# Attention and gated FFN on one core: one group's input sums in five parts, another first bank for the one-unit group, one state copy on VectorE

## The chip, the core and the metric

The kernel runs on one core of one Trainium2 chip. The metric is device time in microseconds (us) of one execution. Five engines work side by side, each in the order of its own instruction list: TensorE (PE in the profile, its weight loads PEld), VectorE (DVE), ScalarE (ACT), GpSimd (POOL) and SyncE (SP), which here only issues DMAs. They wait for each other through semaphores. An engine that waits holds up everything behind it in its list.

## The reference

A causal linear attention with decay, in blocks of 64 positions, for 4 batches, 8 heads, 768 positions and a head size of 64:

```python
for b in range(nb):
    intra = einsum(qb, kb) * Dmask[None]            # scores inside the block, decayed and masked
    intra = einsum(intra, vb)
    inter = einsum(qb * lam_pow[None], kv_state)    # all earlier blocks, through a 64 x 64 state
    out[:, :, sl] = intra + inter
    kv_state = lam_block * kv_state + einsum(kb * rev_pow, vb)
```

Its output, as a matrix x of 3072 tokens by 512, goes through a gated layer with 1536 hidden columns:

```python
a = x @ w_a
b = x @ w_b
return (a * b @ w_out)
```

All inputs are drawn at random in float32, and the output is float32.

## The kernel before

**Units and groups.** A unit is 128 tokens of one batch with all heads; there are 24, six to a batch. They are taken in eight groups of 4, 1, 2, 4, 4, 4, 4 and 1 units (`GROUPS`). The attention of a unit writes its result, transposed and in bf16, into a tile `xT` of its group; the gated layer of a group reads that tile. While the layer of group g runs, the attention of later units is slipped in between its matmuls: after each step the layer calls `hook(slot)`, and the table `PLAN[g]`, written by hand, says which pieces are emitted at which slot. There is no other scheduler: each engine works in the order in which the code emits.

**Pieces.** `P` prepares a unit (scaling of q and k on POOL, the transposing DMA, v to bf16), `S` its scores and masks, `V` updates the running state, `O2` makes the outputs of two units and copies them to `xT` in two halves on ScalarE (`evac_o`, L520: the first copy writes two of the four blocks of 128 rows, the second the others). For later pairs `O2` also updates the state beside it (`kv_beside`, L549) and copies it for the next unit (`kv_copy`): on VectorE as one multiply with a block mask (L560), or on ScalarE as two copies (L558); the table `KV_ENG` says which. `X` makes the sums of a group's x (`x_sums`, L701).

**The layer of groups 3 to 6.** It uses a Strassen-like scheme with seven products of half size in place of eight (`ffn_z`). They need sums of quarters of x: `z_sub` (1024 columns per partition), `z_add` (1024) and `z_mix` (512), made once per group, and sums of the weights. For each of six steps n, products are accumulated in PSUM banks named U (bank 0 or 1 in turn), V and W; ScalarE copies two or three partial results out (`snap`, L812), VectorE subtracts them from later ones (L760 to L777), a last product into U follows in the next step, ScalarE copies it (L737) and VectorE multiplies the two factors (L739, tile `ab`). In group 3 a step begins: U from `xT`, V from the first half of `z_sub`, W from the first half of `z_add`, then U from `z_mix` (which must wait until the first U has been copied), then V from the other half of `z_add`. In groups 5 and 6 the output products of the group before are slipped in too (`H`, L853; their input sums are `SM`, L826 to L832), and V and W share a bank. The sums of group 6 (`X`, 6) are made by POOL.

**The output of group 3** is plain (`out_plain`, L793): four tiles, each copied by ScalarE into one of the three buffers of `o_pool` (L638) and stored by a DMA that SyncE issues (L639).

**SyncE's list** holds in emission order the loads of q, k and v (L187), the transposing DMAs (L429) and the stores.

**Banks.** PSUM has eight banks; one holds the state. `ps_bank` hands out the others in rotation from a counter `bank["next"]`, leaving out those in `bank["held"]`. While groups 3 to 6 run, banks 0 to 4 are held, and 5 and 6 serve the attention. The last group, one unit, uses the ordinary layer `ffn` (`a_part` and `b_part`: tiles a_ps and b_ps, L596) in rotation over banks 0, 1, 2, 5 and 6, while 3 and 4 take the output products of group 6. Just before it the pending last product of group 6 is emitted:

```python
            bank["held"] = {3, 4} if fin else set()
            if fin:
                fin.pop()()
            ffn(g_u0[g], n, gx.pop(g), hook, g == 0, g + 1 == len(GROUPS))
```

Of the kernel before, what the change touches and what calls it, by code (L numbers as in the profile page):

```python
# [17 lines left out]
BF16 = mybir.dt.bfloat16  # L18
# [4 lines left out]
def _bc(ap, dims):  # L23
# [58 lines left out]
Z_GROUPS = (3, 4, 5, 6)  # L82
# [10 lines left out]
                        [0] +  # L93
                        [1] +
                        [0] * 2))
KV_ENG = dict(enumerate(["dve"] * 10 + ["act"] * 2 + ["dve"] + ["act"] * 11))
VB_ENG = dict(enumerate(["pool"] * 7 +
                        ["dve"] * 3 +
                        ["pool"] * 5 +
# [14 lines left out]
def kernel(  # L114
# [11 lines left out]
    nc = tc.nc  # L126
# [20 lines left out]
    xz_pool = ctx.enter_context(tc.tile_pool(name="xz", bufs=4))  # L147
# [11 lines left out]
    bank = {"next": 0, "held": set(), "ffn": None}  # L159
# [12 lines left out]
    def z_bank(name, i):  # L172
        return ps_pool.tile([128, 2, 256], F32, name=name, tag=f"ps{i}")
# [57 lines left out]
    def cast_w(kind, c, eng):  # L231
        t, slot = staged.pop((kind, c))
        if slot is not once:
            slots.append(slot)
        if kind == "o":
            dst = wo_sb[:, 2 * c:2 * c + 2, :]
        else:
            dst = w_part(wa_sb if kind == "a" else wb_sb, c)
        if eng == "act":
            nc.scalar.copy(dst, t)  # L240
        elif eng == "pool":
            nc.gpsimd.tensor_copy(dst, t)
        elif eng == "first":
            nc.vector.tensor_copy(dst[:, :3, :128], t[:, :3, :128])  # L244
            nc.gpsimd.tensor_copy(dst[:, 3:, :128], t[:, 3:, :128])
            nc.gpsimd.tensor_copy(dst[:, :, 128:], t[:, :, 128:])
        elif eng == "both":
            nc.vector.tensor_copy(dst[:, :, :128], t[:, :, :128])
            nc.scalar.copy(dst[:, :, 128:], t[:, :, 128:])
        elif eng == "cols":  # L250
            nc.vector.tensor_copy(dst[:, :, :128], t[:, :, :128])
            nc.vector.tensor_copy(dst[:, :, 128:], t[:, :, 128:])
        else:
            nc.vector.tensor_copy(dst, t)
        pump()
# [73 lines left out]
    gx, xTs = {}, {}  # L329
    g_u0 = [sum(GROUPS[:i]) for i in range(len(GROUPS))]  # L330

    def new_xT(g):
        gx[g] = xT_pool.tile([128, KS, 512], BF16, name="xT", tag="xT")
        for i in range(GROUPS[g]):
            xTs[g_u0[g] + i] = (gx[g], i * BLK)
# [61 lines left out]
    def eng_of(name):  # L397
        return nc.gpsimd if name == "pool" else nc.vector
# [35 lines left out]
    def prep_v(u):  # L434
        make_vb(u, VB_ENG[u])
        pump()
# [116 lines left out]
    def kv_copy(u, ps, eng="dve"):  # L553
        st = st_bufs[u % 4]
        if eng == "act":
            for b in range(2):
                p = slice(64 * b, 64 * b + 64)
                nc.scalar.copy(st[p, :, b, :], ps[p, :, b, :])  # L558
        else:
            nc.vector.tensor_mul(st[:].rearrange("p c b d -> p c (b d)"),  # L560
                                 ps[:].rearrange("p c b d -> p c (b d)"), bdiag_bc)

    def piece_S(u):
        masks(u, scores(u))

    def piece_V(u):
        kv_update(u)
        if u % NB < NB - 1:
            kv_copy(u, kv["ps"], KV_ENG[u])

    def pieces_O(us, nxt=()):
# [15 lines left out]
        if beside and us[1] % NB < NB - 1:  # L587
            kv_copy(us[1], kv["ps"], KV_ENG[us[1]])

# [37 lines left out]
    def store_kept():  # L627
        row, o_sb = kept.pop(0)
        nc.sync.dma_start(out=out_r[row], in_=o_sb)
# [68 lines left out]

    xz = {}

    def x_sums(g):  # L701
        xT = gx[g]
        z_add = xz_pool.tile([128, 2, 512], BF16, name="z_add", tag="xz")
        z_sub = xz_pool.tile([128, KS, 256], BF16, name="z_sub", tag="xz")
        z_mix = mix_pool.tile([128, 2, 256], BF16, name="z_mix", tag="z_mix")
        eng_of(XS_ENG[g, 0]).tensor_sub(z_sub, xT[:, :, 0:256], xT[:, :, 256:512])
        eng_of(XS_ENG[g, 1]).tensor_add(z_add, xT[:, 0:2, :], xT[:, 2:4, :])
        eng_of(XS_ENG[g, 2]).tensor_add(z_mix, xT[:, 0:2, 0:256], xT[:, 2:4, 256:512])
        xz[g] = (z_add, z_sub, z_mix)

    fin = []
    pairs = [0]
# [97 lines left out]
    def snap(ps):  # L810
        t = snap_pool.tile([128, 2, 256], F32, name="u", tag="snap")
        nc.scalar.copy(t, ps)  # L812
        return t
# [22 lines left out]
    def out_half(g, i):  # L836
        d = outs[g]
        p, h = O_ORDER[i // 2], i % 2
        ab = d["ab"]
        lhs = {0: ab[:, NP:, 256:], 1: ab[:, :NP, 256:], 2: ab[:, NP:, :256], 4: ab[:, :NP, :256]}  # L840
        if p in (3, 5, 6):
            lhs[p] = d["z"][:, 1 if p == 6 else 0]
        rhs = wo_sums.get(p)
        if rhs is None:
            rhs = wo_sb[:, :NP, :HN] if p == 1 else wo_sb[:, NP:, HN:]
        c = "U" if p in (1, 5, 3, 2) else "V"
        fresh = h == 0 and p in (4, 1, 0)
        if fresh:
            d[c] = z_bank("op", 3 if c == "U" else 4)
        ps = d[c]  # L850
        for n in range(h * NP // 2, (h + 1) * NP // 2):
            for t in range(2):
                nc.tensor.matmul(ps[:, t, :], lhsT=lhs[p][:, n, t * 128:(t + 1) * 128],  # L853
                                 rhs=rhs[:, n, :], start=fresh, stop=True, skip_group_check=True)
                fresh = False
        if h:
            if p in (4, 1, 5):
                d[{4: "v1", 1: "u1", 5: "u2"}[p]] = snap(ps)
            else:
                o = o_pool.tile([128, 2, 256], F32, name="o_sb", tag="osb")  # L860
                if p == 2:
                    nc.scalar.copy(o, ps)
                else:
                    nc.vector.tensor_sub(o, ps, d[{6: "u2", 3: "v1", 0: "u1"}[p]])
                r, cc = {2: (0, 0), 3: (0, 1), 0: (1, 0), 6: (1, 1)}[p]
                rows = out_r[d["u0"] + 2 * r:d["u0"] + 2 * r + 2, :, cc * HN:(cc + 1) * HN]
                nc.sync.dma_start(out=rows.rearrange("t p n -> p t n"), in_=o)
# [130 lines left out]
    for g, n in enumerate(GROUPS):  # L998
        if g + 1 < len(GROUPS):
            new_xT(g + 1)  # L1000
        plan = {}
        for slot, name, us in PLAN.get(g, ()):
            plan.setdefault(slot, []).append((name, us))

        def hook(slot, plan=plan):
            for name, us in plan.get(slot, ()):
                if name == "C":
                    cast_w("o", us, CO_ENG[us])
                elif name == "PK":
                    prep_k(us)  # L1010
                elif name == "PV":
                    prep_v(us)
                elif name == "P":
                    prep_k(us)
                    prep_v(us)
                elif name == "W":
                    store_kept()
                elif name == "WS":
                    weight_sum(us)
                elif name == "WO":  # L1020
                    out_sum(us)
                elif name == "SM":
                    ab_sum(*us)
                elif name == "H":
                    out_half(*us)
                elif name == "X":
                    x_sums(us)
                elif name == "T":
                    piece_T(us)
                elif name == "S":  # L1030
                    piece_S(us)
                elif name == "VC":
                    kv_copy(us, kv["ps"], KV_ENG[us])
                elif name == "V":
                    piece_V(us)
                elif name == "O":
                    pieces_O((us,))
                elif name == "O2":
                    pieces_O(us)
                else:  # L1040
                    pieces_O(us[:2], us[2:])

        if g in Z_GROUPS:
            bank["held"] = set(range(5))
            joined = any(name == "H" and us[0] < g for slot, name, us in PLAN[g])
            own = any(slot >= 18 for slot, name, us in PLAN[g])
            ffn_z(g, g_u0[g], gx.pop(g), hook, joined, own)
        else:
            bank["held"] = {3, 4} if fin else set()
            if fin:  # L1050
                fin.pop()()
            ffn(g_u0[g], n, gx.pop(g), hook, g == 0, g + 1 == len(GROUPS))

# [28 lines left out]
```

## Time and profile before

| | |
|---|---|
| time, median of 3 runs | 225.81 us (225.62 to 226.88) |
| the profiled execution: its time | 225.77 us |
| the profiled execution: its span | 224.0 us |
| mean granted TensorE clock | 0.999 of full |
| busy share of the span | PE 95%, PEld 71%, DVE 73%, ACT 55%, POOL 45% |
| DMA | 39.42 MB, 176 GB/s in the mean |

The span reaches from the first instruction to the last that the profile shows; the profiled execution's time is 1.77 us longer. All times in the views are in us from the span's start. A matmul's end is modelled, so starts of matmuls tell more than their busy time. The stages, from the windows view (length; then for each engine busy us and, in brackets, instructions; granted clock; mean DMA share; GB/s):

```profile
82.50:86.70 4.20, 3.40 (x31) 2.11 (x26) 2.88 (x4) 3.15 (x7) 2.59 (x3) 1.00 1.11 209
86.70:97.00 10.30, 10.30 (x123) 8.63 (x123) 9.62 (x16) 7.66 (x15) 6.03 (x6) 1.00 1.28 220
...
112.00:119.00 7.00, 7.00 (x42) 3.46 (x42) 5.41 (x7) 3.63 (x9) 4.16 (x4) 1.00 1.23 238
...
170.00:182.00 12.00, 11.86 (x119) 10.04 (x116) 7.86 (x12) 8.39 (x18) 9.25 (x5) 1.00 0.07 24
```

The engines stand in the order PE, PEld, DVE, ACT, POOL. Group 3's products start at 83.84, group 4's at 118.24, group 5's near 139, group 6's at 174.15, and the last group's layer at 203.09.

### The profile page before, as it was taken

The numbers are of one execution on the slowest core, as the hardware profiler recorded it, in microseconds if no ns is written. First come the engines' busy times: TensorE is split into PE (matmuls) and PEld (weight loads), VectorE is DVE, ScalarE is ACT, GpSimd is POOL, SyncE is SP. The second block draws the span as 40 slices with busy tenths as digits, with TensorE's granted clock in tenths as the row PEclk, the third lists the DMA queues.
The fourth block names the chain that finished last, engine by engine and source line by source line (L and its number), as shares of the span: only waits on it lengthen the run. The fifth ranks groups of instructions, "written<-read, shape, count | busy, mean of one in ns | idle before, by whom it ended". The sixth has DMA issues, their size and how long they took to land.

```text
span 224.0 us, 5599 instructions
## 1 busy us (share of the span) xinstructions
PE 213.6 (95%) x2225; PEld 159.0 (71%) x2235; DVE 163.5 (73%) x269; ACT 123.4 (55%) x251; POOL 100.2 (45%) x95
## 2 busy tenths in 40 slices
PE   7797999999999998999999999899999999999994
PEld 2374444448778756887547888688888888888994
DVE  0994763988798659889977979968686765776440
ACT  2684556018554156675366988776536665533322
POOL 6061004346794076542249369786427722052000
PEclk9999999999999999999999999999999999999999
DMA  4999999999999999999999999752021100112042
GB/s 128 322 253 349 357 387 340 272 221 208 218 187 220 233 188 245 190 281 231 154 247 219 224 220 230 145 94 50 0 96 47 51 0 4 47 52 91 0 143 94
DMA packets 99081, 39.42 MB, mean 176 GB/s; under 512 B 85488, under 2 KB 95088, under 8 KB 99056
## 3 DMA queue, kind: packets, MB, share of 16 engines
q1 hardware_dynamic: 98768, 39.00, 79.2%
q8 instruction: 17, 0.28, 0.6%
q10 hardware_dynamic: 288, 0.07, 0.1%
q14 instruction: 8, 0.07, 0.1%
HBM read 28.32 MB, written 6.29 MB: 154 GB/s over the span
## 4 chain that ended last, share of the span: by engine, by line
PE 86%; DMA 5%; SPq 3%; ACT 2%; DVE 2%; issue 1%; ACTq 0%
PE U L731 18%; PE op L853 12%; PE b_ps L596 10%; PE a_ps L596 9%; PE V L731 9%; PE op L643 9%; PE W L731 5%; PE op L793 5%; PE o_ps L497 4%; DMA wst<-in_moe_w_a_dram 3%; PE kq L457 3%; SPq L187 2%; DMA q<-in_q_dram 2%; PE kvd L527 1%; ACT xT L520 1%
## 5 line engine op out<-in xcount | busy, mean ns | idle before, releaser
L812 ACT COPY u<-U 128x512 f32<-128x512 f32 x48 | 28.4, 591 | 16.4 <-PE U L731 16.2
L401 POOL TENSOR_TENSOR qk<-kf,lp_k 128x512 bf16<-128x512 f32 x18 | 20.7, 1148 | 35.2 <-DMA kf<-in_k_dram 22.1
L623 DVE TENSOR_TENSOR ab<-a_sb,b_ps 128x128 bf16<-128x128 bf16 (+2 forms) x48 | 19.3, 417 | 16.4 <-PE b_ps L596 7.8
L596 PE MATMUL a_ps<-xT,wa_sb 128*128 128x128 bf16 (+2 forms) x198 | 27.6, 267 | 1.6 <-DVE wa_sb L244 1.3
L480 DVE TENSOR_TENSOR m<-kq,lotri 128x512 bf16<-128x512 f32 x40 | 25.7, 683 | 4.2 <-PE kq L457 4.2
L596 PE MATMUL b_ps<-xT,wb_sb 128*128 128x128 bf16 (+2 forms) x192 | 27.5, 272 | 0.5 <-ACT oab L737 0.5
L739 DVE TENSOR_TENSOR ab<-oab 128x1024 bf16<-128x1024 bf16 x24 | 18.4, 766 | 11.7 <-ACT oab L737 11.6
L605 ACT CAST a_sb<-a_ps 128x128 bf16<-128x128 f32 (+2 forms) x48 | 17.3, 375 | 16.7 <-PE a_ps L596 14.8
L401 POOL TENSOR_TENSOR qk<-qf,lp_q 128x512 bf16<-128x512 f32 x20 | 24.5, 1227 | 1.9 <-DMA qf<-in_q_dram 1.9
L643 PE MATMUL op<-wo_sb,ab 128*128 128x512 bf16 (+2 forms) x114 | 21.8, 334 | 0.5 <-issue 0.3
L596 PEld LDWEIGHTS <-wa_sb 128*128 128x128 bf16 x200 | 16.7, 98 | 7.7 <-DVE wa_sb L244 1.5
L731 PEld LDWEIGHTS <-wz_a 128*128 128x128 bf16 x192 | 18.2, 98 | 3.6 <-issue 0.5
L596 PEld LDWEIGHTS <-wb_sb 128*128 128x128 bf16 x192 | 15.7, 98 | 6.6 <-issue 0.6
L731 PEld LDWEIGHTS <-wz_b 128*128 128x128 bf16 x192 | 18.8, 98 | 2.2
L731 PE MATMUL U<-xT,wz_a 128*128 128x256 bf16 x96 | 18.3, 272 | 0.0
L731 PE MATMUL U<-xT,wz_b 128*128 128x256 bf16 x96 | 18.3, 272 | 0.0
L520 ACT CAST xT<-o_ps 128x512 bf16<-128x512 f32 (+1 forms) x24 | 12.2, 556 | 10.7 <-PE o_ps L497 10.5
L731 PEld LDWEIGHTS <-wa_sb 128*128 128x128 bf16 x144 | 13.4, 98 | 4.7 <-issue 2.0
L770 DVE TENSOR_TENSOR oab<-U,u 128x512 bf16<-128x512 f32 x24 | 16.4, 682 | 0.4 <-PE U L731 0.4
L643 PEld LDWEIGHTS <-ab 128*128 128x128 bf16 x120 | 10.2, 98 | 8.5
L737 ACT CAST oab<-U 128x512 bf16<-128x512 f32 x24 | 14.2, 591 | 3.5 <-PE U L731 3.5
L420 POOL CAST vb<-vf 128x512 bf16<-128x512 f32 x14 | 9.7, 695 | 13.4 <-DMA vf<-in_v_dram 12.5
(126 smaller groups left out, 451.9 us busy)
## 6 DMA issues: line engine op xcount, KB each, us to landing
vf<-in_v_dram SPq DMA_DIRECT2D x24, 256.0 KB, 5.1
qf<-in_q_dram SPq DMA_DIRECT2D x20, 256.0 KB, 4.5
kf<-in_k_dram SPq DMA_DIRECT2D x20, 256.0 KB, 4.7
out_dram<-o_sb SPq DMA_DIRECT2D x18, 256.0 KB, 2.4
wst<-in_moe_w_a_dram SPq DMA_DIRECT2D x6, 512.0 KB, 8.6
wst<-in_moe_w_b_dram SPq DMA_DIRECT2D x6, 512.0 KB, 9.1
wst<-in_moe_w_out_dram SPq DMA_DIRECT2D x6, 512.0 KB, 10.6
out_dram<-o_kept SPq DMA_DIRECT2D x5, 256.0 KB, 4.3
```

What stands on the lines that cost most here:

```text
L401: eng_of(eng).tensor_mul(dst.rearrange("p (c b) d -> p b c d", b=2), x[:].rearrange("p (b c) d -> p b c d", b=2), lp.rearrange("p (b c) o ...
L480: nc.vector.tensor_mul(m, kq[i], lotri_bc)
L520: nc.scalar.copy(dst, src)
L596: nc.tensor.matmul(ps[:, lo:hi], lhsT=w_sb[:, s, f * 128:(f + 1) * 128], rhs=xT[:, s, lo:hi], start=(s == 0), stop=(s == KS - 1), skip_gro ...
L605: nc.scalar.copy(a_sb[:, :gt], ps[:, :gt])
L623: nc.vector.tensor_mul(ab[:, f, :gt], a_sb[:, :gt], ps[:, :gt])
L643: nc.tensor.matmul(op[:, lo:hi], lhsT=ab[:, f, t * 128:(t + 1) * 128], rhs=wo_sb[:, f, lo:hi], start=(f == 0), stop=(f == FC - 1))
L731: nc.tensor.matmul(ps[:, k, :], lhsT=wt[:, s, n * 128:(n + 1) * 128], rhs=rhs[i][:, s, :], start=(fresh and k == 0 and s == 0), stop=True, ...
L739: nc.vector.tensor_mul(ab[:].rearrange("p (h i) (t c) -> p h i t c", h=2, t=2)[:, :, n], o5[:, :, :, 0, :], o5[:, :, :, 1, :])
L770: nc.vector.tensor_sub(oab[:, 1], U, v1)
L812: nc.scalar.copy(t, ps)
L853: nc.tensor.matmul(ps[:, t, :], lhsT=lhs[p][:, n, t * 128:(t + 1) * 128], rhs=rhs[:, n, :], start=fresh, stop=True, skip_group_check=True)
```

## The change

Three edits.

1. The sums of group 3. They become five VectorE instructions of 512 columns each. The first, half of `z_add` over the first two units, is a new piece `XA`, emitted at the same slot as the group's last `O2` and ahead of it. The other four come at the place of `X`, in another order: first half of `z_sub`, `z_mix`, second half of `z_add`, second half of `z_sub`.
2. The counter of the banks is set to 5 before the one-unit group, so that its first two tiles take banks 5 and 6; before, they took 0 and 1, and U of group 6's last step is in bank 1.
3. The state after unit 22 (piece `O2` of units 21 and 22, in group 5) is copied by VectorE (one L560) instead of ScalarE (two L558).

On TensorE the order of instructions stays the same, and on POOL and SyncE everything does.

```diff
-        (13, 'W', None), (13, 'V', 9), (14, 'O2', (9, 10)), (14, 'X', 3), (15, 'W', None)],
+        (13, 'W', None), (13, 'V', 9), (14, 'XA', 3), (14, 'O2', (9, 10)), (14, 'X', 3), (15, 'W', None)],
...
-KV_ENG = dict(enumerate(["dve"] * 10 + ["act"] * 2 + ["dve"] + ["act"] * 11))
+KV_ENG = dict(enumerate(["dve"] * 10 + ["act"] * 2 + ["dve"] + ["act"] * 9 + ["dve", "act"]))
...
+    def x_add_first(g):
+        x_first[g] = x_tile()
+        nc.vector.tensor_add(x_first[g][:, :, 0:256], gx[g][:, 0:2, 0:256], gx[g][:, 2:4, 0:256])
+
     def x_sums(g):
         xT = gx[g]
-        z_add = xz_pool.tile([128, 2, 512], BF16, name="z_add", tag="xz")
+        z_add = x_first.pop(g) if g in x_first else x_tile()
+        add_half = lambda c: nc.vector.tensor_add(z_add[:, :, c], xT[:, 0:2, c], xT[:, 2:4, c])
         z_sub = xz_pool.tile([128, KS, 256], BF16, name="z_sub", tag="xz")
         z_mix = mix_pool.tile([128, 2, 256], BF16, name="z_mix", tag="z_mix")
+        xz[g] = (z_add, z_sub, z_mix)
+        if g == Z_GROUPS[0]:
+            sub = lambda s: nc.vector.tensor_sub(z_sub[:, s], xT[:, s, 0:256], xT[:, s, 256:512])
+            sub(slice(0, 2))
+            nc.vector.tensor_add(z_mix, xT[:, 0:2, 0:256], xT[:, 2:4, 256:512])
+            add_half(slice(256, 512))
+            sub(slice(2, 4))
+            return
         eng_of(XS_ENG[g, 0]).tensor_sub(z_sub, xT[:, :, 0:256], xT[:, :, 256:512])
...
+                elif name == "XA":
+                    x_add_first(us)
...
             bank["held"] = {3, 4} if fin else set()
             if fin:
+                bank["next"] = 5
                 fin.pop()()
```

More of the change, by code (lines that the diff above doesn't have):

```diff
@@ L699, with x_tile @@
     xz = {}
+    x_first = {}
+    def x_tile():
+        return xz_pool.tile([128, 2, 512], BF16, name="z_add", tag="xz")
+    def x_add_first(g):
+        x_first[g] = x_tile()
+        nc.vector.tensor_add(x_first[g][:, :, 0:256], gx[g][:, 0:2, 0:256], gx[g][:, 2:4, 0:256])
     def x_sums(g):
         xT = gx[g]
-        z_add = xz_pool.tile([128, 2, 512], BF16, name="z_add", tag="xz")
+        z_add = x_first.pop(g) if g in x_first else x_tile()
+        add_half = lambda c: nc.vector.tensor_add(z_add[:, :, c], xT[:, 0:2, c], xT[:, 2:4, c])
         z_sub = xz_pool.tile([128, KS, 256], BF16, name="z_sub", tag="xz")
         z_mix = mix_pool.tile([128, 2, 256], BF16, name="z_mix", tag="z_mix")
+        xz[g] = (z_add, z_sub, z_mix)
[6 more added lines that the diff above has]
+            return
         eng_of(XS_ENG[g, 0]).tensor_sub(z_sub, xT[:, :, 0:256], xT[:, :, 256:512])
@@ L708, in x_sums @@
         eng_of(XS_ENG[g, 2]).tensor_add(z_mix, xT[:, 0:2, 0:256], xT[:, 2:4, 256:512])
-        xz[g] = (z_add, z_sub, z_mix)
     fin = []
```

## The prediction

> **What bounds the kernel now.** I read the chain of waits first: the work that ended last, followed back.
>
> ```profile
> PE 86%; DMA 5%; SPq 3%; ACT 2%; DVE 2%; issue 1%; ACTq 0%
> ```
>
> TensorE carries it. From 85.7 us to the end other engines appear on it at three places only (near 140.0, 170.5 and 203.3 us). So an edit pays where TensorE waits, and the gain lasts only until TensorE meets something that does not move with it. I read the timeline at the three places that the change touches, and then searched for that something.
>
> Place one, the start of group 3's products, where a line is start, duration, instruction, and in brackets the idle time before it and who ended it:
>
> ```profile
> 83.40 1.21 DVE L706 TENSOR_TENSOR z_sub<-xT 128x1024 bf16<-128x1024 bf16 x1 [2.40 <-ACT xT L520]
> ...
> 84.54 1.09 DVE L707 TENSOR_TENSOR z_add<-xT 128x1024 bf16<-128x1024 bf16 x1
> 84.67 0.38 PE L731 MATMUL V<-z_sub,wa_sb 128*128 128x256 bf16 x2 [0.23 <-DVE z_sub L706]
> ...
> 85.56 0.41 DVE L708 TENSOR_TENSOR z_mix<-xT 128x512 bf16<-128x512 bf16 x1
> 85.68 0.38 PE L731 MATMUL W<-z_add,wa_sb 128*128 128x256 bf16 x2 [0.42 <-DVE z_add L707]
> ```
>
> VectorE has been idle for 2.40 us, then the sums come one after the other and TensorE waits for two of them. Place two, the end of group 5 (unit 22's state and what follows):
>
> ```profile
> 169.61 0.69 DVE L777 TENSOR_TENSOR oab<-W,u 128x512 bf16<-128x512 f32 x1 [0.57 <-PE W L731]
> ...
> 169.69 0.75 ACT L558 CAST st<-kvd 64x256 bf16<-64x256 f32 x2
> ...
> 170.46 0.59 ACT L812 COPY u<-U 128x512 f32<-128x512 f32 x1
> ...
> 171.10 0.38 PE L731 MATMUL U<-z_mix,wz_a 128*128 128x256 bf16 x2
> ```
>
> ScalarE copies the state for 0.75 us while a finished U waits for its copy u, and the next product into U waits for that copy. Place three, the start of the one-unit group:
>
> ```profile
> 203.34 0.59 ACT L737 CAST oab<-U 128x512 bf16<-128x512 f32 x1 [0.41 <-PE U L731]
> ...
> 203.97 0.38 PE L596 MATMUL b_ps<-xT,wb_sb 128*128 128x128 bf16 x4 [0.49 <-ACT oab L737]
> ```
>
> The first b_ps falls into the bank that ScalarE is still reading. Last, the start of group 4, which the change does not touch:
>
> ```profile
> 114.14 1.02 SPq L639 DMA_DIRECT2D out_dram<-o_sb  x1
> ...
> 118.76 0.59 ACT L638 COPY o_sb<-op 128x512 f32<-128x512 f32 x1 [2.32 <-DMA out_dram<-o_sb]
> ...
> 119.25 0.59 ACT L812 COPY u<-U 128x512 f32<-128x512 f32 x1
> ...
> 119.99 0.38 PE L731 MATMUL U<-z_mix,wz_a 128*128 128x256 bf16 x2
> ```
>
> ScalarE stands 2.32 us waiting until the store of output tile 0 has landed (o_pool has three buffers, this is the fourth tile). The copy of U queues behind it and ends at 119.84; the product that needs it starts at 119.99. Nothing stalls yet, but only 0.11 us is spare (a released product starts some 0.04 us after its releaser, as 85.68 after 85.63).
>
> **The change, part by part.** Four products into a bank issue in 0.44 us (the pieces of the chain), so I work with starts.
>
> The sums. Group 3's three sums (1024, 1024 and 512 elements) become five of 512. The first, a half of z_add, is put ahead of the outputs of units 9 and 10. Its data, units 7 and 8, were copied out by 79.53; VectorE is free from 81.00 to 83.40 and POOL is idle from 80.76 to 82.03. At 0.41 us (z_mix above) it is hidden; even at 1.26, the longest sum of that size in the trace, it would end at 82.3. No VectorE instruction and no DMA is queued between its place and the other sums. Its buffer, from the pool of the a_sb tiles, was last read by VectorE itself near 76 us. Then come z_sub's first half (it needs the first of the two xT copies), z_mix, z_add's other half and z_sub's rest. U starts at 83.84, so V can start at 84.28 instead of 84.67 and W at 84.72 instead of 85.68: 0.96 us. The next product needs z_mix and the copy u that ends at 85.12, so it goes at 85.16, also 0.96 earlier. z_sub's first half must end by 84.24 and z_mix by 85.1. Collisions with POOL bound their cost: 0.41 alone, 1.26 beside a POOL multiply. POOL is busy until 85.08 here, and z_sub's 1024 took 1.21 instead of the 0.69 of the other groups, so I take 0.6 to 0.7 each: the half ends by 84.1, z_mix by 84.8. At this place the gain is 0.85 to 0.96 us.
>
> It does not last. VectorE had 2.0 us of idle time from 86 to 113 us and its work moves along; the transposes land 1.3 us or more ahead of their scores. But the store at 114.14 stands in SyncE's queue, which has no gap over 0.15 us from 80.24 to 120.85: transposes, loads and stores in fixed order, with the DMA engines full. TensorE's earliness does not move it. It lands 4.5 us later, so ScalarE copies U no sooner than 119.25, and the product cannot start before 119.88. TensorE then waits some 0.8 us at 119 instead of 0.96 at 84 to 86. What is left is 119.99 - 119.88 = 0.11 us.
>
> The state of unit 22. ScalarE loses two copies (0.75), VectorE gains one multiply with the block mask (0.68, the group of L560). ScalarE can then copy U when it is done, 170.04 instead of 170.46, and the product at 171.10 follows straight on V. VectorE's multiply waits for the state's matmuls, which end at 169.03, and runs 169.08 to 169.76; queued behind it is L777, which goes from 169.61 to 169.69, and V, which waits for it in the same bank, from 170.35 to about 170.43. So the product goes from 171.10 to 170.87 at best: 0.23. The new state is read at 175.12, 5 us later. What is late next: POOL's sums for group 6 start with the xT copies at 169.8, which do not move, and VectorE's sums collide with them. L739 at 171.57 took 0.98 instead of 0.69 and ended 0.54 after POOL's z_sub (172.01); asked for 0.4 earlier it would end no earlier. The same holds for the sum L830 behind it (0.85 instead of 0.55, ended 0.42 after POOL's z_add). So L777 stays at 174.87 to 175.56, and group 6's first V, which waits for it, can go from 175.70 only to 175.60. I take 0.10. The bounds are 0.23 gained, if those sums do move, and 0.37 lost, if the multiply put its whole 0.68 on V less the 0.31 that TensorE idles there anyway.
>
> The Trainium skill ("SBUF — State Buffer", section "SBUF: two separate sides") says that VectorE, in a sum of two SBUF operands, and GpSimd hold their shared ports as an exclusive lock for a whole instruction. The two pairs of rows agree, and by that rule the term is 0.10; by a mere sharing of speed it would be nearer 0.23 and the sum 224.84.
>
> The banks. Setting the counter to 5 gives the first a_ps and b_ps banks 5 and 6, which nothing reads since 176 us, and b_ps loses its wait: 203.31 instead of 203.97, 0.66. Next, output products follow; the last two matmuls of the second half need the ab that VectorE finishes at 204.65. They would start at 204.63 and so wait 0.07. The sum a21 (L828, done 205.91) is needed at 206.01: in time. Later banks come round in the same distance of five. Gain 0.59; bounds 0 and 0.66.
>
> The sum, on the profiled execution's own 225.77 us (span 224.0 and 1.77 around it; the median of the runs is 225.81): 225.77 - 0.11 - 0.10 - 0.59 = 224.97.
>
> **The rivals.** First: the earliness of group 3 survives. If the store lands earlier, each tenth is a tenth gained, up to 0.85; then 225.77 - 0.96 - 0.10 - 0.59 = 224.1. For it: the three stores of these tiles took 3.9 to 5.2 us to land, and 3.9 instead of 4.5 alone would give 224.4. Against it: the full SyncE queue, and that a late landing (5.2) holds up both kernels, to 225.6 in the changed one.
>
> Second: the bank edit gives nothing, because the output products wait for the last ab instead. 225.77 - 0.21 = 225.56. Against it, the 0.07 worked out above.
>
> Third, slower: the four sums after the xT copies each run into a POOL instruction. At 1.26 each they end at 83.40 + 5.04 = 88.44 instead of 85.97. Then L760, two masks and L770 of the first step come 2.05 later; L770 ends at 91.2, and the product that it frees a bank for, at 89.61 before, comes 1.6 late. With 119.88 no longer deciding: 225.77 + 1.6 - 0.10 - 0.59 = 226.7. It begins to cost from about 0.8 us a sum. For it: one sum of 512 took 1.26. Against it: POOL has nothing to do from 85.08 to 87.20, so at most the first two can collide.
>
> **How the numbers follow.** Forecast 0.58, first rival 0.28, second 0.08, third 0.06. One run in five lies outside 224.1 to 225.7: the first rival's end below, and above the forecast with a late store or the second rival. About 0.5% (1.13 us, to 224.68) is what a measurement of this kernel can tell from no change. Faster by more: the first rival's 0.28 and 0.07 of the forecast's spread, 0.35. Slower by over 0.5% needs 226.94, the third rival with a second mishap: 0.05. The rest, 0.60, is within.
>
> **What would show it.** Right: W at about 84.7 with no wait; a new wait of some 0.8 us before U<-z_mix near 119.9, still ended by the copy behind L638; no L558 and one more L560 near 169; b_ps straight behind a_ps near 203. Wrong: L638 after its store's landing clearly before 118.5 (first rival); the same 0.5 us wait a step later near 204 (second); DVE sums of over 0.8 us from 83 to 86 with L760 later than 86.39 (third).

## The result, and the profile after

The changed kernel takes 224.03 us (median of 17 runs, 223.34 to 225.84), against 225.81 us (17 runs) of the kernel before: a ratio of 0.9939, 95% interval 0.992 to 0.9959. The ratios use fast runs alone (two slow ones of the kernel before, 229.65 and 231.45 us, are left out here), the medians all runs. Two repetitions on other occasions gave 0.9954 (0.9929 to 0.9979) and 0.9949 (0.9918 to 0.9979). Its profiled execution took 223.83 us, with a span of 222.1 us; the forecast for it was 224.97. Lines of the code stand some 17 further down than before: products L748, copies `snap` L829, masks and differences L777 to L794, input sums L843 to L849, output products L870.

The line of the chain of waits, by engine:

```profile
PE 67%; DMA 16%; SPq 5%; DVE 5%; ACT 2%; issue 2%; POOL 1%; ACTq 0%; DVEq 0%; POOLq 0%
```

TensorE's share falls from 86% to 67%. That is not a slower DMA: the chain, followed back, now leaves TensorE at 88.7 us and goes back through a store and SyncE's list. Here is that spot of the chain, in order of time (start, duration, piece):

```profile
79.79 1.55 SPq L429
...
82.64 1.04 SPq L187
...
83.72 4.32 DMA out_dram<-o_kept
...
88.11 0.59 ACT u L829
```

The kept outputs (`o_kept`, tiles of the first groups whose store is put off to a later slot, `W` in the table) lie in `snap_pool`, the pool that also holds the copies u. The third of them is stored by SyncE behind unit 11's transpose and unit 13's loads. Its buffer is free only when the store has landed, 4.32 us after its issue, and a copy u of group 3's second step wants it. The same spot in the kernel before, the issue of that store, the copy, and the product that waits for the copy:

```profile
84.19 1.19 SPq L629 DMA_DIRECT2D out_dram<-o_kept  x1
...
88.98 0.59 ACT L812 COPY u<-V 128x512 f32<-128x512 f32 x1
...
90.05 0.38 PE L731 MATMUL V<-z_add,wz_a 128*128 128x256 bf16 x2
```

The store took 4.53 us there and landed at 88.71, only 0.27 us before the copy began.

The timeline at place one. VectorE, ScalarE and TensorE:

```profile
80.06 0.41 DVE L708 TENSOR_TENSOR z_add<-xT 128x512 bf16<-128x512 bf16 x1
...
82.07 0.43 DVE L718 TENSOR_TENSOR z_sub<-xT 128x512 bf16<-128x512 bf16 x1 [1.59 <-ACT xT L520]
82.56 1.12 DVE L720 TENSOR_TENSOR z_mix<-xT 128x512 bf16<-128x512 bf16 x1
83.60 0.82 DVE L713 TENSOR_TENSOR z_add<-xT 128x512 bf16<-128x512 bf16 x1
84.35 0.41 DVE L718 TENSOR_TENSOR z_sub<-xT 128x512 bf16<-128x512 bf16 x1
...
88.11 0.58 ACT L829 COPY u<-V 128x512 f32<-128x512 f32 x1 [0.83 <-DMA out_dram<-o_kept]
...
83.87 0.38 PE L748 MATMUL W<-z_add,wa_sb 128*128 128x256 bf16 x2
...
88.75 0.38 PE L748 MATMUL V<-z_add,wz_a 128*128 128x256 bf16 x2 [0.34 <-ACT u L829]
```

V and W have no wait any more, although z_mix took 1.12 us and the second half of z_add 0.82, both while POOL was at work. One step later ScalarE stands 0.83 us for the kept store, and TensorE waits for ScalarE. At the start of group 4, where the prediction put the new wait:

```profile
112.67 0.87 SPq L639 DMA_DIRECT2D out_dram<-o_sb  x1
...
117.24 0.58 ACT L638 COPY o_sb<-op 128x512 f32<-128x512 f32 x1 [2.05 <-PE op L810]
```

ScalarE waits for TensorE there, not for the store, which was issued 1.47 us earlier than before. Place two and place three:

```profile
167.82 0.69 DVE L560 TENSOR_TENSOR st<-kvd,bdiag 128x512 bf16<-128x512 f32 x1
...
169.90 1.40 DVE L756 TENSOR_TENSOR ab<-oab 128x1024 bf16<-128x1024 bf16 x1 [0.79 <-ACT oab L754]
...
168.62 2.13 POOL L724 TENSOR_TENSOR z_sub<-xT 128x1024 bf16<-128x1024 bf16 x1 [1.41 <-ACT xT L520]
...
201.75 0.39 PE L596 MATMUL a_ps<-xT,wa_sb 128*128 128x128 bf16 x4
201.98 0.39 PE L596 MATMUL b_ps<-xT,wb_sb 128*128 128x128 bf16 x4
```

L756 took 1.40 us beside POOL's `z_sub`, and b_ps follows a_ps without a wait.

To see where the time went, I took the weight load of the same TensorE instruction in both traces (the order on TensorE is the same) and followed the shift of its start along the execution:

| weight load of | before, us | after, us | shift |
|---|---|---|---|
| group 3's first U, last pair | 84.06 | 83.21 | -0.85 |
| U from `z_mix`, first step | 86.12 | 84.32 | -1.80 |
| V from `z_add`, second step | 90.05 | 88.75 | -1.30 |
| scores of unit 12 | 91.01 | 89.76 | -1.25 |
| group 4's U from `z_mix` | 119.99 | 118.74 | -1.25 |
| group 6, behind its first V | 176.15 | 174.81 | -1.34 |
| the one-unit group, behind its first steps | 206.16 | 204.25 | -1.91 |

So the 1.9 us of span are 0.85 that this execution was ahead before anything changed had run, 0.40 from the sums (0.95 gained, 0.55 given back by 91 us), 0.09 from the state and 0.57 from the banks. The 0.85 does not belong to the change: by 20 us, in the loads at the start, this execution was 1.38 ahead, of which 0.53 was gone again by 70 us; the same kernel, profiled two more times, was ahead by 0.05 and 0.09 at 84 us.

### The profile page after: what moved, and what is told of

Read it like the earlier page. It is cut to its first block, busy times and chain, and to the rows that moved or that the text cites. A ratio compares the mean times of both kernels' runs of the same rounds, so it can differ in the third digit from the quotient of the medians.

```text
span 222.1 us, 5601 instructions
## 1 busy us (share of the span) xinstructions
PE 213.9 (96%) x2225; PEld 159.0 (72%) x2235; DVE 165.3 (74%) x272; ACT 122.7 (55%) x249; POOL 99.8 (45%) x95
## 4 chain that ended last, share of the span: by engine, by line
PE 67%; DMA 16%; SPq 5%; DVE 5%; ACT 2%; issue 2%; POOL 1%; ACTq 0%; DVEq 0%; POOLq 0%
PE U L748 17%; PE op L870 12%; PE V L748 9%; DMA wst<-in_moe_w_b_dram 8%; PE b_ps L596 5%; PE op L810 5%; PE a_ps L596 5%; PE W L748 4%; PE op L643 3%; DMA kf<-in_k_dram 3%; DMA k<-in_k_dram 3%; PE o_ps L497 3%; PE kq L457 2%; DMA out_dram<-o_kept 2%; SPq L187 1%
## 5 line engine op out<-in xcount | busy, mean ns | idle before, releaser
L829 ACT COPY u<-U 128x512 f32<-128x512 f32 x48 | 28.3, 590 | 16.5 <-PE U L748 16.4
L401 POOL TENSOR_TENSOR qk<-kf,lp_k 128x512 bf16<-128x512 f32 x18 | 19.5, 1084 | 33.7 <-DMA kf<-in_k_dram 18.9
L756 DVE TENSOR_TENSOR ab<-oab 128x1024 bf16<-128x1024 bf16 x24 | 19.0, 791 | 11.3 <-ACT oab L754 11.1
L748 PEld LDWEIGHTS <-wz_a 128*128 128x128 bf16 x192 | 18.2, 98 | 3.9 <-issue 0.9
L748 PEld LDWEIGHTS <-wz_b 128*128 128x128 bf16 x192 | 18.7, 98 | 2.2
L748 PE MATMUL U<-xT,wz_a 128*128 128x256 bf16 x96 | 18.3, 272 | 0.0
L748 PE MATMUL U<-xT,wz_b 128*128 128x256 bf16 x96 | 18.3, 272 | 0.0
L420 POOL CAST vb<-vf 128x512 bf16<-128x512 f32 x14 | 10.2, 730 | 13.8 <-DMA vf<-in_v_dram 13.8
L748 PEld LDWEIGHTS <-wa_sb 128*128 128x128 bf16 x144 | 13.4, 98 | 4.0 <-issue 1.0
```

Source lines behind the costliest of these rows:

```text
L401: eng_of(eng).tensor_mul(dst.rearrange("p (c b) d -> p b c d", b=2), x[:].rearrange("p (b c) d -> p b c d", b=2), lp.rearrange("p (b c) o ...
L748: nc.tensor.matmul(ps[:, k, :], lhsT=wt[:, s, n * 128:(n + 1) * 128], rhs=rhs[i][:, s, :], start=(fresh and k == 0 and s == 0), stop=True, ...
L756: nc.vector.tensor_mul(ab[:].rearrange("p (h i) (t c) -> p h i t c", h=2, t=2)[:, :, n], o5[:, :, :, 0, :], o5[:, :, :, 1, :])
```

## The experiments

All kernels below have the order of TensorE's instructions in common, so the shifts can be read in every profile as above. Ratios are to the kernel before, run beside each on the same chip. The theories: the landing of the third kept store takes back part of the sums' gain (T), against the prediction's own limit at group 4 and against a price in later loads.

**Each edit alone.** `sums_only` has edit 1, `bank_only` edit 2, `state_only` edit 3.

> Edit 1 alone (five sums, one ahead). Theory: W follows V without a wait (0.96 us saved near 84 to 86), and about half of it is lost near 88.75, where ScalarE's copy of V in step 1 of group 3 waits for a snap buffer whose stored tile o_kept has not landed: net 0.4 to 0.5 us faster than before. Rival A (that loss was one execution's): the full 0.96. Rival B (the prediction as written: the store of group 4's first tile decides): 0.11.

> Edit 2 alone (first banks 5 and 6 in the one-unit group). Theory: b_ps follows a_ps without the wait on the copy L737, 0.66 less 0.07 at the last matmuls of the second half of the output product: 0.57 to 0.59 us faster. Rival: the output products wait for the last ab in its place, and the time is the same.

> Edit 3 alone (unit 22's state by VectorE). Theory: the product U<-z_mix near 171 starts 0.25 earlier, and group 6's first V only 0.10 earlier, since L777 there is held by VectorE's sum beside POOL: 0.1 us faster, hardly told from the same. Rival: the 0.25 stays.

Measured: 226.09 us, ratio 1.0013 (0.9988 to 1.0037); 225.48, 0.9987 (0.9969 to 1.0006); 226.22, 1.0017 (0.9995 to 1.0039). By the time alone none of the three can be told from no change, and the interval of `sums_only` excludes the 0.4 to 0.5 us that were expected of it. The profiles say more. In `bank_only` the shift goes from +0.12 at 203.09 to -0.45 at 206.16: 0.57 again. In `state_only` it goes by 0.09 around 171 us, as in the changed kernel. In `sums_only` 0.94 is gained by 86.12 (+0.13 to -0.81) and 0.61 is left at 91 us (-0.48), with the same waiter:

```profile
88.88 0.58 ACT L829 COPY u<-V 128x512 f32<-128x512 f32 x1 [0.61 <-DMA out_dram<-o_kept]
```

`sums_only` and the three profiles of the changed kernel have the same list on SyncE. The third kept store landed at 88.80, 88.03, 89.59 and 88.75 in them, and V from `z_add` in the second step started at 89.52, 88.75, 90.30 and 89.46: each time 0.71 or 0.72 us behind the landing, however early TensorE had been. In the four profiles with the old sums and the same list (`before`, `bank_only`, `state_only`, `no_sums`) it started 1.30 to 1.39 us behind, and no copy waited for the store.

`state_only` showed something else. Its sums are the old ones, yet TensorE lost 0.68 us more at them than in the kernel before, because POOL's work for unit 12 came later there (it had waited 2.46 us for k) and met the sums instead of preceding them:

```profile
83.06 1.49 POOL L401 TENSOR_TENSOR qk<-kf,lp_k 128x512 bf16<-128x512 f32 x1 [2.46 <-DMA kf<-in_k_dram]
...
83.57 1.53 DVE L707 TENSOR_TENSOR z_add<-xT 128x1024 bf16<-128x1024 bf16 x1
85.02 1.26 DVE L708 TENSOR_TENSOR z_mix<-xT 128x512 bf16<-128x512 bf16 x1
```

**The third kept store earlier in SyncE's list** (`w_early_after`), in the changed kernel:

```diff
-        (6, 'V', 8), (10, 'PK', 10), (11, 'PV', 10), (11, 'P', 11), (11, 'W', None),
+        (6, 'V', 8), (10, 'PK', 10), (11, 'PV', 10), (11, 'W', None), (11, 'P', 11),
```

> The changed kernel, with the third kept store (piece W at slot 11 of group 2) emitted ahead of piece P of unit 11 and not behind it, so that SyncE issues it while it waits for POOL, some 4.5 us earlier, and unit 12's transpose no longer has it in front. Theory (the landing of that store takes half of edit 1's gain): ScalarE's copy of V in step 1 no longer waits for the store, V from z_add in that step starts without a wait, and the time is 0.4 to 0.5 us under that of the changed kernel, about 1.5 to 1.9 us under before. Rival (the DMA engines' full load decides, wherever the store stands): the same time as the changed kernel.

Measured: 225.17 us, 0.9965 (0.9939 to 0.9992). The wait at 88 us was gone, but the transposes of units 11 and 12, now behind the store, came late, and so did the fourth kept store:

```profile
86.34 0.40 PE L457 MATMUL kq<-qkT 64*128 64x128 bf16 x8 [1.27 <-DMA qkT<-qk]
91.11 0.40 PE L457 MATMUL kq<-qkT 64*128 64x128 bf16 x8 [0.33 <-DMA qkT<-qk]
...
102.28 0.59 ACT L829 COPY u<-U 128x512 f32<-128x512 f32 x1 [1.79 <-DMA out_dram<-o_kept]
...
102.92 0.38 PE L748 MATMUL U<-xT,wz_a 128*128 128x256 bf16 x2 [0.97 <-ACT u L829]
```

The shift went from -1.64 at 86.12 to +0.10 at 91 and +1.42 at 119.99. So this run didn't confirm T: it traded one wait for others, and its time can't be told from the changed kernel's. The profiled run took 226.49 us, 1.3 us above the median, so its waits are not those of a typical run.

**All five kept stores early**, in the changed kernel (`w5_after`) and in the one before (`w5_before`): five `W` at slot 2 of group 2, the later ones taken out. Beside them, the changed kernel again (`after_again`) and edits 2 and 3 without 1 (`no_sums`).

> The changed kernel as it is, on the chip of this comparison. If the three edits alone would each do what their stages show (0.4 to 0.6, 0.57 and 0.10 us), it is 1.1 to 1.3 us faster than before. Rival (the whole is less than the first comparison said, since the edits alone came out at the same): 0.5 us or less.

> Edits 2 and 3 without edit 1. Theory: 0.57 + 0.10, so 0.6 to 0.7 us faster than before, and 0.4 to 0.6 slower than the changed kernel. In its trace b_ps follows a_ps at once near 203, group 6's first V is 0.1 earlier against what precedes it, and near 85 W waits for z_add as in the kernel before. Rival (edit 1 is worth its full 0.96): 1 us slower than the changed kernel.

> The changed kernel with all five kept stores (pieces W) at slot 2 of group 2, where two of them stand already; three leave SyncE's list behind unit 11's transpose. Theory (landings of stores and transposes decide what edit 1 keeps): ScalarE's copies in group 3 find their buffers free, SyncE's list is 1 us ahead at unit 12's transpose and 2 to 3 us from unit 14's on, the sums' 0.96 us stays whole until group 4, and the time is 0.4 us or more under the changed kernel's. The price is 2 us later loads of units 11 and 12; if that decides, unit 11's or 12's scores wait for their transpose, and the time is the same or longer (rival).

> The kernel before with the same move of the kept stores. Theory: TensorE waits for the sums there and for no store, so the move gives nothing: within 0.3 us of before. Rival (DMA waits hold the kernel before too, in many executions): 0.5 us faster or more.

Measured: `after_again` 224.82 us, 0.9954 (0.9929 to 0.9979); `no_sums` 225.28, 0.9982 (0.9956 to 1.0007); `w5_after` 226.39, 1.0027 (1.0003 to 1.0051); `w5_before` 226.86, 1.0059 (1.0029 to 1.0089). For `no_sums` the expected 0.6 to 0.7 us lie inside the interval, and its profile shows the 0.09 of the state and the 0.57 of the banks. In `w5_after` the rival holds: stores ahead of the loads cost more than they free. TensorE waited 0.49 and 0.59 us for transposes, and of the 0.95 us gained at the sums nothing was left at 91 us. That profile is of the fastest of the 12 runs; the median is 1.6 us above `after_again`, and no profile shows all of it. `w5_before` fits neither its theory nor its rival: it is 0.9 us slower, with waits of 0.65 and 0.59 us for transposes and a further 0.68 us lost near 107 us.

`w5_before` gave a clue to the sums. Its later loads left POOL idle from 82.03 to 84.28, and the three old sums, undisturbed, took 0.69, 0.68 and 0.42 us:

```profile
82.95 0.69 DVE L706 TENSOR_TENSOR z_sub<-xT 128x1024 bf16<-128x1024 bf16 x1 [2.41 <-ACT xT L520]
83.56 0.68 DVE L707 TENSOR_TENSOR z_add<-xT 128x1024 bf16<-128x1024 bf16 x1
84.16 0.42 DVE L708 TENSOR_TENSOR z_mix<-xT 128x512 bf16<-128x512 bf16 x1
```

No product waited for a sum there, and TensorE was 0.93 us earlier at this place than in the kernel before, without edit 1. So TensorE's 0.96 us in the kernel before is the price of meeting POOL, not of the order of the sums by itself. The five parts meet POOL too (two of them took 1.26 us each in `after_again`), but no product waits for the parts that do: the gain against the kernel before was 0.94 or 0.95 in every profile with edit 1.

`after_again` has the wait for the kept store at its worst:

```profile
90.30 0.38 PE L748 MATMUL V<-z_add,wz_a 128*128 128x256 bf16 x2 [1.09 <-ACT u L829]
...
89.67 0.59 ACT L829 COPY u<-V 128x512 f32<-128x512 f32 x1 [1.58 <-DMA out_dram<-o_kept]
```

The store was issued at 84.96 there and took 4.63 us; 0.95 us were gained at the sums and 1.30 lost again, a net loss of 0.35 in this execution. The sums are not shown to have cost this: the landing at 89.59 and the 0.71 us behind it give 90.30, and the old sums with this start would have put V at 90.00 (90.05 less the 0.05 of the start), so they would have waited 0.30 us too, as an estimate.

**The third kept store issued by ScalarE.** This frees it from SyncE's list without pushing anything in that list back. In the changed kernel (`actq_after`) and, as a control, in edits 2 and 3 alone (`actq_no_sums`), with the changed kernel beside them (`after_third`):

```diff
         row, o_sb = kept.pop(0)
-        nc.sync.dma_start(out=out_r[row], in_=o_sb)
+        (nc.scalar if row == 2 else nc.sync).dma_start(out=out_r[row], in_=o_sb)
```

> The changed kernel, with the third kept store (output tile 2) issued by ScalarE instead of SyncE at the same place of the code; ScalarE reaches it near 75 to 77 us, where it idles 3.04 us in the changed kernel's profile, so it lands near 80 instead of 88. Theory (the landing of that store, in SyncE's full list, takes 0.4 to 1.3 us of the 0.96 that the sums gain): ScalarE's copy u<-V of group 3's second step no longer waits for a kept tile, the shift of TensorE at 91 us equals that at 86 us, and the time is 0.5 to 1.0 us under the changed kernel's in the same call. Rival A (the prediction's own: group 4's store takes it anyway): the wait goes from 88 us to the product U<-z_mix near 119, ended by the copy behind L638, and the time equals the changed kernel's within 0.3. Rival B (the moved bytes push a transpose late, as when SyncE issued that store before unit 11's transpose): TensorE waits for qkT at 81 to 91 us, and the time is 0.3 or more above the changed kernel's.

> Control: the bank edit and the state edit alone (the sums as before), with the third kept store issued by ScalarE. There ScalarE's copy waited for no kept store, so the theory expects no change against the bank and state edits alone (ratio to before 0.996 to 0.999), and actq_after 0.8 to 1.0 us under it. Rival A: actq_after at most 0.4 under it. Rival B: above the bank and state edits alone, by the waits for qkT.

> The changed kernel again, as the yardstick of this call. Theory and both rivals: 0.9939 to 0.9954 of before, with ScalarE's copy u<-V waiting 0.4 to 1.6 us for the third kept store near 88 us.

Measured: 224.07 us, 0.9933 (0.9903 to 0.9962); 225.42, 0.9986 (0.9953 to 1.0018); 224.32, 0.9949 (0.9918 to 0.9979). In `actq_after` the copy u<-V no longer waits for a store; the wait comes back at the next kept store, which is still SyncE's:

```profile
74.58 0.34 ACTq L629 DMA_DIRECT2D out_dram<-o_kept  x1
...
87.56 0.59 ACT L829 COPY u<-V 128x512 f32<-128x512 f32 x1
...
100.11 0.59 ACT L829 COPY u<-U 128x512 f32<-128x512 f32 x1 [1.14 <-DMA out_dram<-o_kept]
...
100.74 0.38 PE L748 MATMUL U<-xT,wz_a 128*128 128x256 bf16 x2 [0.32 <-ACT u L829]
...
117.92 0.59 ACT L638 COPY o_sb<-op 128x512 f32<-128x512 f32 x1 [2.38 <-DMA out_dram<-o_sb]
```

The shift stays at -1.43 from 86 to 99 us (the whole 0.95 kept), falls to -0.89 by 105 us, and the start of group 4 takes nothing, although ScalarE waits 2.38 us for the store there. With the 0.71 to 0.72 us above, this settles that the third kept store takes back the gain at 88 us. The whole time is not shown to be better than the changed kernel's: 224.07 against 224.32 us, with intervals that overlap, where 0.5 to 1.0 us was expected. In the profile the fourth kept store took 0.54 back.

In the control's profile the old sums met POOL's late work, as in `state_only`, and TensorE lost 0.68 us more at them than in the kernel before. Its time is as expected, and `actq_after` is 1.35 us under it, where 0.8 to 1.0 was expected.

**The last three kept stores issued by ScalarE** (`actq3_after`): `row >= 2` in the line above, and the last `W` moved so that two come at slot 13, ahead of the last `O2`.

> The changed kernel, with the last three kept stores (output tiles 2, 3 and 4) issued by ScalarE: tile 2 at the same place, tiles 3 and 4 after ScalarE's copy of the output tile that ends near 80.2 us, where it idles 1.63 us. With tile 2 alone moved, the 0.96 us held to 99 us, and then 0.54 went in a wait of ScalarE's u<-U (1.14 us) for the next kept store. Theory (the kept stores are what takes the gain of the sums): no wait for a kept tile from 84 to 115 us, the shift of TensorE at 113 us equals that at 86 us, and the time is 0.990 to 0.994 of before. What is next: ScalarE's copy of output tile 3 (L638) waits for the first store of group 3, whose issue moves up by the issue time of two stores (about 1.5 us), so that U<-z_mix near 119 loses nothing or at most 0.3. Rival (the DMA engines are full, so what moves ahead pushes q, k and v of units 11 and 12 back): TensorE waits for qkT or kf at 84 to 95 us, and the time is 0.996 or more of before. The prediction's own limit: the shift is lost at U<-z_mix near 119, 0.5 us or more.

Measured: 224.96 us, 0.9973 (0.9943 to 1.0003). The rival holds. No copy waited for a kept store any more, but the transpose of unit 11, issued at 79.28 among these stores, held SyncE for 3.12 us and landed 7.34 us after its issue (2.08 and 4.96 in the changed kernel's first profile), and TensorE waited:

```profile
86.67 0.40 PE L457 MATMUL kq<-qkT 64*128 64x128 bf16 x8 [1.63 <-DMA qkT<-qk]
```

The shift fell from -1.68 to +0.02 at this one place. So behind the kept stores the transposes are the next limit in this profile, and what was moved ahead of their landing was paid there.

The shift of TensorE in the profiles of kernels with the new sums, in us:

| kernel | 84.06 | 86.12 | 91.01 | 119.99 | what took it |
|---|---|---|---|---|---|
| changed | -0.85 | -1.80 | -1.25 | -1.25 | third kept store |
| `after_again` | -0.05 | -1.00 | +0.30 | +0.30 | third kept store |
| `after_third` | -0.09 | -1.03 | -0.54 | -0.54 | third kept store |
| `sums_only` | +0.13 | -0.81 | -0.48 | -0.48 | third kept store |
| `actq_after` | -0.48 | -1.42 | -1.43 | -0.89 | fourth kept store |
| `actq3_after` | -0.73 | -1.68 | +0.02 | +0.11 | transpose of unit 11 |
| `w_early_after` | -0.69 | -1.64 | +0.10 | +1.42 | transposes, then kept and output stores |
| `w5_after` | -0.72 | -1.67 | -0.46 | -0.36 | transposes |

## Why the prediction came out as it did

It said 225.0 us, with a range of 224.1 to 225.7; the medians of the changed kernel were 224.03, 224.82 and 224.32. The first lies 0.07 below the range, the other two inside it. A gain of over 0.5% was given 0.35 and a smaller one or none 0.60; the ratios stand for 0.61, 0.46 and 0.51%, right at that line.

**The banks: right.** 0.59 was forecast, 0.57 measured, and the same within 0.01 us in every profile with edit 2. The second rival falls: no wait of 0.5 us came a step later.

**The state: right, for the reason given.** 0.10 was forecast, 0.09 measured. L756 was asked for earlier, took 1.40 us instead of 0.98, and ended 0.55 us after POOL's `z_sub` (171.30 against 170.75), where before it had ended 0.54 after it. The rule of the Trainium skill ("SBUF — State Buffer", section "SBUF: two separate sides"), by which VectorE and GpSimd hold their shared ports as an exclusive lock, agrees with this: started 0.4 us earlier, the instruction won nothing.

**The sums at their place: right.** 0.85 to 0.96 was forecast, 0.95 measured, and 0.94 or 0.95 in all the other profiles with edit 1. Sums beside POOL were bounded at 1.26 us; the longest took 1.12 here and 1.26 in `after_again`, and both hid.

**"It does not last": the step that failed.** The term was 0.11; the four profiles with SyncE's list unchanged show 0.40, 0.45, 0.61 and -0.35. Two things were wrong in it. First, the search for the next limit looked at the transposes and the store at 114.14, and missed the buffers that the copies u share with the kept outputs. That limit bites at 88 us, 31 us sooner. The rows of the kernel before had its size: the third kept store landed at 88.71, a copy begins some 0.09 us after a landing (118.76 after 118.67), takes 0.59, and the product starts 0.04 later, at 89.43 instead of 90.05. So 0.62 us could be kept, not 0.11, as an estimate, and the sum would have been 224.46. The announced wait of 0.8 us before U<-`z_mix` near 119.9 is in none of the four, and in only one profile of all (`w_early_after`, 0.13 us) was anything lost there. Second, it took the issue of the store at 114.14 for fixed by the list ahead of it to a tenth. In the three profiles of the changed kernel it was issued at 112.67, 113.32 and 114.91. In the second, as in `sums_only` (113.38), SyncE stood waiting for the end of the store's own copy (113.30, 113.36), so that the store moved along with TensorE; in the first the list reached it just as the copy ended (112.58); only in the third did the list come 0.77 us after the copy (114.14), as it came 0.30 after it before. One profile without a gap in SyncE's list was read as a list that never has one: in the first profile of the changed kernel SyncE waited 0.48 us before the transpose at 108.28. A term of 0.1 cannot be read from a limit that moves by 2 us between executions.

**The first rival** (the earliness survives, 224.1) is nearest in number to 224.03, and half right in mechanism: a part survives, and its sign, L638 before 118.5, came in three of the four profiles (117.24, 117.95 and 118.01; 118.99 in `after_again`). But that the number came so near was in part luck. In the sum for the profiled execution, 224.97 less 223.83 is 1.14, of which 0.85 is the start-up and 0.29 the sums; the state and the banks came 0.03 short, and 0.03 lie behind the last row of the table (1.94 us of time against a shift of 1.91). The sum of the three effects read in this profile is 0.40 + 0.09 + 0.57 = 1.06 us, and the three measured ratios stand for 1.4, 1.0 and 1.1 us.

**The third rival** (four sums each collide with POOL) didn't come about: two of the four did, at 1.12 and 0.82 us, and no product waited for them.

**What stays open.** The times of the single edits do not add up to that of all three: their ratios multiply to 1.0017, with about 0.004 of uncertainty, against 0.9939 to 0.9954. `no_sums` to `after_again`, on one chip, makes the sums worth 0.6 us, with intervals that overlap, but the time of `sums_only` excludes a gain of over 0.3. In the profiles the sums' net value against the kernel before runs from a loss of 0.35 to a gain of 0.61 with the landing of the third kept store, and what the old sums lose varies too, from nothing to 1.6 us. Either may be the reason; one profile per kernel can't show it. The changed kernel was not run on the chip of the single edits, so a difference between chips is not excluded. What sets the lateness of SyncE's list, and the start-up's spread, was not tried.

## What to carry to other kernels

Before a gain at one place is booked, follow every buffer that the earlier instructions will ask for, those of a shared pool above all: the spare time of its oldest tenant (here 0.27 us behind a store of 4.53 us) is the next limit. A limit set by a full DMA list should be booked as a range over its issue times in several executions, not as one number. And a wait that looks like an order of instructions may be two engines meeting: look at the same instructions in an execution where they don't.

## What the hardware showed that I had not expected

- The same VectorE sum of 1024 columns took 0.68, 1.09 and 1.53 us, and the one of 512 columns 0.41 to 1.26, with what POOL ran beside it. Whether they meet can hang on the landing of a k load, for which POOL waited 2.46 us in `state_only`, and TensorE's loss at the old sums went from nothing (`w5_before`) through 0.96 to 1.6 us (`state_only`).
- The transposing DMA of unit 11 held SyncE for 2.08, 2.20 and 2.26 us in the three profiles of the changed kernel, for 2.76 in `actq_after` and for 3.12 in `actq3_after`, and a store issued by ScalarE at 74.58 held ScalarE only 0.34 us, while SyncE's issues from 72 to 84 us in that profile took 0.57 to 2.76 us.
- At 84 us, ahead of all that edits 1 to 3 move on TensorE, the profiles stand between 0.89 us ahead of that of the kernel before (`no_sums`) and 0.13 behind it (`sums_only`): more than any single edit here is worth.
